# Probability-times-value matmuls in turn between two PSUM banks, in an attention and feed-forward kernel

## The chip, the cores and the metric

The kernel runs on one core of one Trainium2 chip. The metric is the device time of one execution in microseconds (us). Several executions of each kernel were timed; all that have a known state were in the fast state, with a granted TensorE clock of 0.997 to 1.000. Single looks on one core have the state "unknown", and nothing below rests on their total time alone.

## The reference

The reference is one transformer block with modulated layer norms, sliding-window attention over a cache, and a gated feed-forward part. All inputs are bfloat16. Cut to what matters:

```
h = layernorm(x) * (1 + ca) + sa                 # x: 2048 x 1024
q = h @ wq                                        # 32 heads of 128
k, v = last 512 rows of the caches                # 4 groups, 8 heads share one
p = softmax(q @ k.T / sqrt(128))                  # per head: 2048 x 512
x = x + ga * ((p @ v) @ wo)
x = x + gb * feed_forward(layernorm(x) * (1 + cb) + sb)
```

The change touches only `p @ v`. The kernel handles 512 query rows at a time, so there are 4 x 32 = 128 pieces of work, called heads below.

## The kernel before

Per head, the exponentials of the scores lie in SBUF as `ex_s`, 4 key tiles of 128 keys x 512 queries. The values lie in `v_aug`: for each group of heads four slices (one per key tile), each a row of 128 values and a column of ones. The column of ones makes the 129th output column the sum of the exponentials. A row is 130 elements long, of which a matmul reads 129.

```python
VW = 130
v_aug = arena.at(OFF_VA, [GK, VW], BF16, [B_va])        # GK = 16 slices: 4 groups x 4
...
T.op(POOL, lambda: g.memset(v_aug[:, :, P:VW], 1.0), writes=[B_va])
...
def pv(i):
    ...
    for j in range(TPC):                                 # 4 blocks of 128 queries
        b = PVB + j // 2                                 # bank 5, 5, 6, 6
        for kt in range(KT):                             # 4 v slices, added up in PSUM
            mm(bank(b, P + 1, (j % 2) * 130), ex_s[es][:, kt, j * P:(j + 1) * P],
               v_aug[:, gk * KT + kt, 0:P + 1],
               kt == 0, kt == KT - 1, [B_ex[es], B_va, B_vg[gk]], PB[b])
    both = [PB[PVB], PB[PVB + 1]]
    # VectorE: reciprocal of the four sums, then one multiplication over both banks
    ...
```

The second argument of `mm` is the stationary operand (weights, loaded anew for each matmul: the trace before has 7778 weight loads and 7636 matmuls, a few matmul records being missing) and the third the moving operand, here a v slice. The two flags say "overwrite" (first of a block) and "last of a block". Both banks are waited for and drained together, before and after the change.

In the loop over heads, TensorE does for one head the query projection (8 matmuls of 512 columns), for another the scores (4 of 512 columns), and for a third these 16 matmuls of 129 columns.

The softmax here doesn't subtract the row's maximum and nothing guards it: scores larger than these inputs give would overflow.

Of the kernel before, what the change touches and what calls it, by code (L numbers as in the profile page):

```python
# [7 lines left out]
P = 128  # L8
# [122 lines left out]
def bass_adaLN_cond__sliding_block_cached__swiglu_ffn__prompt_kernel(  # L131
# [23 lines left out]
    KT = W // P  # L155
# [3 lines left out]
    TPC = CH // P  # L159
# [57 lines left out]
    def bank(b, n=512, off=0):  # L217
        return ps[:, b * 512 + off:b * 512 + off + n]
# [7 lines left out]
    def psap(off, dims):  # L226
        return bass.AP(tensor=ps_t, offset=off, ap=[[4096, P]] + dims)

    PB = [_Buf("bank%d" % b) for b in range(8)]
# [23 lines left out]
    PVB = 5  # L253
    XB = 7

    with nc.Block() as block:

        @block.gpsimd
        def _(g):
# [5 lines left out]
            def mm(out_ap, lhsT, rhs, start, stop, reads, bank_buf, skip=False):  # L265
                T.op(PE, lambda: TE.matmul(out_ap, lhsT, rhs, start=start, stop=stop, skip_group_check=skip),  # L266
                     reads=reads, writes=[bank_buf])
# [98 lines left out]
            v_aug = arena.at(OFF_VA, [GK, VW], BF16, [B_va])  # L366
            Q_k = [dq("q_k%d" % i) for i in range(Hkv)]
            Q_v = [dq("q_v%d" % i) for i in range(Hkv)]
            B_vg = [_Buf("vg%d" % i) for i in range(Hkv)]
# [217 lines left out]
            for idx in range(GK):  # L587
                b = SCB + 1 + idx // 8
# [18 lines left out]
            B_ex = [_Buf("ex%d" % i) for i in range(NEX)]  # L607
            ex_s = [arena.at(OFF_EX + i * 4 * KB, [KT, CH], BF16, [B_ex[i]]) for i in range(NEX)]
# [14 lines left out]
            def pv(i):  # L623
                ch, h = divmod(i, Hq)
                gk = h // rep
                es = i % NEX
                os_ = i % NOS
                for j in range(TPC):
                    b = PVB + j // 2
                    for kt in range(KT):  # L630
                        mm(bank(b, P + 1, (j % 2) * 130), ex_s[es][:, kt, j * P:(j + 1) * P], v_aug[:, gk * KT + kt, 0:P + 1],
                           kt == 0, kt == KT - 1, [B_ex[es], B_va, B_vg[gk]], PB[b])
                both = [PB[PVB], PB[PVB + 1]]
                r = i % 2
                T.op(DVE, lambda: V.reciprocal(rl[r][:, :].rearrange("p (a b) -> p a b", a=2), psap(PVB * 512 + P, [[512, 2], [130, 2]])),  # L635
                     writes=both + [B_rl[r]])
                rlb = bass.AP(tensor=rl[r][:, :].tensor, offset=0, ap=[[4, P], [2, 2], [1, 2], [0, P]])
                T.op(DVE, lambda: V.tensor_tensor(o_s[os_].rearrange("p (a b) d -> p a b d", a=2),  # L638
                                                  psap(PVB * 512, [[512, 2], [130, 2], [1, P]]), rlb, ALU.mult),
                     reads=[B_rl[r]], writes=both + [B_os[os_]])  # L640
                T.op(Q_tr[os_], lambda: SP.dma_start_transpose(oT_all[:, h, :].rearrange("p (j q) -> p j q", j=TPC),
                                                               o_s[os_].rearrange("p j d -> p (j d)")),
                     reads=[B_os[os_]], writes=[B_oT[h]])
# [55 lines left out]
            for i in range(1, NA + 2):  # L699
# [35 lines left out]
                if 0 <= i - 2 < NA:  # L735
                    pv(i - 2)
                    ch2, h2 = divmod(i - 2, Hq)
                    if h2 == Hq - 1 and ch2 < NCH - 1:
                        finish(rows)
                        oproj(ch2)  # L740
# [144 lines left out]
```

## Time and profile before

| | before |
|---|---|
| time, median | 1291.36 us (3 executions, 1290.51 to 1291.66; the profiled one took 1292.6) |
| TensorE busy | 1265.6 of 1290.8 us |
| 2048 matmuls of 129 columns, busy | 140.6 us |
| heads apart | 3.52 us |

The page of the profile before, its first line, the busy times, and the line of the chain that ended last (shares of the span by engine). In the views that follow, L266 is the helper that issues nearly all matmuls:

```profile
span 1290.8 us, 17912 instructions
...
PE 1265.6 (98%) x7636; PEld 651.7 (50%) x7778; DVE 447.7 (35%) x823; ACT 341.3 (26%) x384; POOL 37.3 (3%) x94
...
PE 97%; issue 1%; DVE 1%; ACT 0%; DMA 0%; SPq 0%; POOL 0%; ACTq 0%
```

The groups of instructions by shape, before. The columns after the bar are busy us in total and mean ns of one, then the idle time of the engine before them:

```profile
L266 PE MATMUL ps<-arena 128*128 128x512 bf16 x5084 | 1134.8, 380 | 10.9 <-DVE arena L467 2.2 <-ACT arena L620 0.6 <-DVE tmp L657 0.4
L266 PEld LDWEIGHTS ps<-arena 128*128 128x128 bf16 x7346 | 637.4, 98 | 624.9 <-issue 7.9 <-ACT arena L620 1.6 <-DVE tmp L657 0.9
...
L266 PE MATMUL ps<-arena 128*128 128x129 bf16 x2048 | 140.6, 220 | 1.1 <-DVE arena L638 1.1
```

The timeline before, VectorE alone, the reciprocals of three heads in a row (start us, duration us):

```profile
403.46 0.18 DVE L635 RECIPROCAL rl<-ps 128x4 f32<-128x4 f32 x1 [1.10 <-PE ps L266]
...
406.98 0.18 DVE L635 RECIPROCAL rl<-ps 128x4 f32<-128x4 f32 x1 [1.10 <-PE ps L266]
...
410.50 0.18 DVE L635 RECIPROCAL rl<-ps 128x4 f32<-128x4 f32 x1 [1.10 <-PE ps L266]
```

What to see: TensorE is the bound, and the 129-column matmuls waited for another engine once, for 1.1 us in all. So whatever they cost is inside their own stream. Their mean duration of 220 ns says nothing of their cost, because matmuls overlap (their starts, below, are only 55.8 to 60.8 ns apart); 140.6 us / 2048 = 69 ns is nearer, but still has the tail of each run of 16 in it. What a matmul costs in a stream is the distance from its start to the next start.

These distances are worked out from the matmul records of the trace, as a mean over the 128 heads (for the last position, without the heads after which the record of the next matmul is missing from the trace). Each number is the distance from the matmul named to the next one, in ns; b is the bank and v the slice:

```
before   b5v0 b5v1 b5v2 b5v3 | b5v0 b5v1 b5v2 b5v3 | b6v0 b6v1 b6v2 b6v3 | b6v0 b6v1 b6v2 b6v3 | sum
         56.6 60.8 59.3 59.3 | 55.8 59.7 59.2 59.6 | 55.8 59.6 59.2 59.2 | 55.8 59.2 59.2 59.1 | 937.4
```

The 512-column matmuls are 215.8 ns apart. The first of each four is followed sooner than the others, by about 3.4 ns.

### The profile page before, as it was taken

To read this page: it belongs to the slowest core of one execution; us is meant where nothing else is said; L and a number is where in the kernel's file an instruction comes from. 1 tells how busy PE (TensorE), PEld (TensorE's weight loads), DVE (VectorE), ACT (ScalarE), POOL (GpSimd) and SP (SyncE) were. 2 spreads that over 40 slices of the span, in tenths; PEclk is the share of its full clock that TensorE was granted. 3 is DMA by queue.
4 is the path that set the end of the run, shared out by engine and by line. 5 is a ranking of instruction groups with operands and counts; after the bars stand their busy time and mean duration, and the time that the engine had idled before them with its cause. 6 is when DMAs were issued, how large, how long until landed. Compare 5 with 4: busy or idle time off the path is not lost.

```text
span 1290.8 us, 17912 instructions
## 1 busy us (share of the span) xinstructions
PE 1265.6 (98%) x7636; PEld 651.7 (50%) x7778; DVE 447.7 (35%) x823; ACT 341.3 (26%) x384; POOL 37.3 (3%) x94
## 2 busy tenths in 40 slices
PE   6999999999999999999999999999999999999999
PEld 3565545556445564456544444444444444444444
DVE  3455423654136542265422332233222331221222
ACT  2555402555015551055620111001100111001100
POOL 1001200000000000000000000000000000000000
PEclk9999999999999999999999999999999999999999
DMA  8989800844105541046340683045420564044300
GB/s 261 304 222 285 235 1 21 184 111 107 37 5 127 133 118 46 1 116 122 70 152 15 205 302 131 17 130 162 151 71 19 157 208 131 17 135 142 131 9 25
DMA packets 212592, 155.33 MB, mean 120 GB/s; under 512 B 104736, under 2 KB 199840, under 8 KB 211488
## 3 DMA queue, kind: packets, MB, share of 16 engines
q1 hardware_dynamic: 212512, 154.17, 42.4%
q8 instruction: 61, 1.00, 0.3%
q14 instruction: 19, 0.16, 0.0%
HBM read 125.83 MB, written 4.19 MB: 101 GB/s over the span
## 4 chain that ended last, share of the span: by engine, by line
PE 97%; issue 1%; DVE 1%; ACT 0%; DMA 0%; SPq 0%; POOL 0%; ACTq 0%
PE ps L266 97%; DMA x_res<-in_A_x_dram 0%; ACT arena L620 0%; PE ps L270 0%; DVE tmp L657 0%; DVE arena L467 0%; DVE st L388 0%; ACT L620 0%; ACT arena L489 0%; SPq L309 0%; DVE nsc L399 0%; DVE arena L638 0%; DVE x_res L659 0%; ACT arena L593 0%; DVE rl L635 0%
## 5 line engine op out<-in xcount | busy, mean ns | idle before, releaser
L266 PE MATMUL ps<-arena 128*128 128x512 bf16 (+1 forms) x7204 | 1251.5, 333 | 12.0 <-DVE arena L467 2.2
L266 PEld LDWEIGHTS ps<-arena 128*128 128x128 bf16 x7346 | 637.4, 98 | 624.9 <-issue 7.9
L620 ACT ACTIVATE arena<-ps 128x1024 bf16<-128x1024 f32 x256 | 261.7, 1023 | 358.9 <-PE ps L266 347.2
L815 ACT ACTIVATE arena<-ps 128x512 bf16<-128x512 f32 x112 | 66.9, 597 | 514.5 <-PE ps L266 511.6
L816 DVE TENSOR_TENSOR arena<-ps,arena 128x512 bf16<-128x512 f32 x112 | 77.5, 692 | 276.2 <-PE ps L266 276.2
L657 DVE TENSOR_TENSOR tmp<-ps,rowb 128x512 f32<-128x512 f32 (+1 forms) x65 | 44.4, 683 | 320.5 <-PE ps L266 320.5
L571 DVE CAST arena<-ps 128x512 bf16<-128x512 f32 x124 | 85.8, 692 | 65.5 <-PE ps L266 65.5
L638 DVE TENSOR_TENSOR arena<-ps,rl 128x512 bf16<-128x512 f32 x128 | 88.5, 691 | 4.4
L635 DVE RECIPROCAL rl<-ps 128x4 f32<-128x4 f32 x128 | 23.4, 183 | 149.7 <-PE ps L266 149.7
L388 DVE BATCH_NORM_STATS2 st<-x_res 128x6 f32<-128x512 bf16 x62 | 42.4, 684 | 4.3 <-DMA x_res<-in_A_x_dram 4.2
L393 POOL TENSOR_SCALAR rstd<-mv 128x1 f32<-128x1 f32 x31 | 7.0, 227 | 955.2 <-DVE mv L392 943.7
L659 DVE TENSOR_TENSOR arena<-tmp,x_res 128x512 bf16<-128x512 f32 (+1 forms) x33 | 22.3, 676 | 1.1
L659 DVE TENSOR_TENSOR x_res<-tmp,x_res 128x512 bf16<-128x512 f32 x32 | 22.1, 692 | 1.1
L404 DVE TENSOR_SCALAR arena<-arena,gain,mod_bf 128x512 bf16<-128x512 bf16 x56 | 20.4, 406 | 0.0
L395 POOL TENSOR_TENSOR rstd<-rstd,mhalf 128x1 f32<-128x1 f32 x31 | 17.7, 572 | 2.6
L399 DVE TENSOR_SCALAR nsc<-x_res,mv,rstd 128x1024 bf16<-128x1024 bf16 x30 | 16.1, 536 | 2.1 <-POOL rstd L395 2.1
L270 PE MATMUL ps<-arena,nsc 128*128 128x128 bf16 x16 | 2.1, 311 | 10.4 <-DVE nsc L399 10.2
L266 PEld LDWEIGHTS ps<-sc_bf,arena 128*128 128x128 bf16 x384 | 11.3, 97 | 0.5
L266 PE MATMUL ps<-sc_bf,arena 128*128 128x1 bf16 x384 | 11.5, 164 | 0.0
L540 POOL TENSOR_SCALAR arena<-arena,c 128x128 bf16<-128x128 bf16 x16 | 9.7, 621 | 36.0 <-PE ps L266 35.9
L392 DVE BATCH_NORM_AGGREGATE mv<-st 128x2 f32<-128x12 f32 x31 | 6.5, 209 | 1.1
L270 PEld LDWEIGHTS ps<-arena,nsc 128*128 128x128 bf16 x16 | 1.5, 142 | 10.4 <-DVE nsc L399 10.4
(37 smaller groups left out, 30.9 us busy)
## 6 DMA issues: line engine op xcount, KB each, us to landing
arena<-in_A_wq_dram SPq DMA_DIRECT2D x31, 1024.0 KB, 5.9
arena<-in_B_w_gate_dram SPq DMA_DIRECT2D x28, 1024.0 KB, 5.3
arena<-in_B_w_up_dram SPq DMA_DIRECT2D x28, 1024.0 KB, 7.4
arena<-in_w_mod_dram SPq DMA_DIRECT2D x8, 1024.0 KB, 7.2
arena<-in_A_wo_dram SPq DMA_DIRECT2D x8, 1024.0 KB, 8.2
arena<-in_B_w_down_dram SPq DMA_DIRECT2D x7, 1024.0 KB, 6.3
arena<-in_w_mod_dram SPq DMA_DIRECT2D x8, 512.0 KB, 7.8
out_dram<-arena SPq DMA_DIRECT2D x15, 256.0 KB, 2.0
```

Of the source, the lines that this page charges most:

```text
L266: T.op(PE, lambda: TE.matmul(out_ap, lhsT, rhs, start=start, stop=stop, skip_group_check=skip), reads=reads, writes=[bank_buf])
L388: T.op(DVE, lambda: V.bn_stats(st_[sl][:, hf * 6:hf * 6 + 6], x_res[:, t, hf * 512:hf * 512 + 512]), reads=[B_x[t]], writes=[B_st[sl]])
L395: T.op(POOL, lambda: g.tensor_tensor(rstd[sl][:, :], rstd[sl][:, :], mhalf[:, 0:1], ALU.pow), reads=[B_rs[sl], B_mh], writes=[B_rs[sl]])
L404: T.op(DVE, lambda: V.tensor_scalar(dst[:, dt, :], dst[:, dt, :], gain[gi][:, dt:dt + 1], mod_bf[:, ccol + dt:ccol + dt + 1], op0=ALU.mult ...
L571: T.op(DVE, lambda: V.tensor_copy(qT_s[qs], bank(QB)), writes=[PB[QB], B_qT[qs]])
L620: T.op(ACT, lambda: A.activation(ex_s[es][:, 2 * kp:2 * kp + 2, :], banks2(SCB + 2 * kp), AF.Exp, scale=att_scale), writes=[PB[SCB + 2 * k ...
L635: T.op(DVE, lambda: V.reciprocal(rl[r][:, :].rearrange("p (a b) -> p a b", a=2), psap(PVB * 512 + P, [[512, 2], [130, 2]])), writes=both + ...
L638: T.op(DVE, lambda: V.tensor_tensor(o_s[os_].rearrange("p (a b) d -> p a b d", a=2), psap(PVB * 512, [[512, 2], [130, 2], [1, P]]), rlb, A ...
L657: T.op(DVE, lambda: V.tensor_tensor(tmp[s][:, 0:n], bank(b, n), rowb[ri][:, c0:c0 + n], ALU.mult), reads=[B_row[ri]], writes=[PB[b], B_tmp ...
L659: T.op(DVE, lambda: V.tensor_tensor(dst[:, c0:c0 + n], tmp[s][:, 0:n], x_res[:, t, c0:c0 + n], ALU.add), reads=[B_tmp[s], B_x[t]], writes= ...
L815: T.op(ACT, lambda: A.activation(sg_s[ss], bank(gb), AF.Silu), writes=[PB[gb], B_sg[ss]])
L816: T.op(DVE, lambda: V.tensor_tensor(guT[:, ft, :], bank(ub), sg_s[ss], ALU.mult), reads=[B_sg[ss]], writes=[PB[ub], B_gu[ft]])
```

## The change

Its intent is to keep a matmul from adding onto the block that the matmul just before it wrote. Now two blocks, in bank 5 and in bank 6, are added to in turn.

```diff
-                for j in range(TPC):
-                    b = PVB + j // 2
+
+                for jj in range(2):
                     for kt in range(KT):
-                        mm(bank(b, P + 1, (j % 2) * 130), ex_s[es][:, kt, j * P:(j + 1) * P], v_aug[:, gk * KT + kt, 0:P + 1],
-                           kt == 0, kt == KT - 1, [B_ex[es], B_va, B_vg[gk]], PB[b])
+                        for jb in range(2):
+                            j = 2 * jb + jj
+                            b = PVB + jb
+                            mm(bank(b, P + 1, jj * 130), ex_s[es][:, kt, j * P:(j + 1) * P], v_aug[:, gk * KT + kt, 0:P + 1],
+                               kt == 0, kt == KT - 1, [B_ex[es], B_va, B_vg[gk]], PB[b])
```

There is a side effect: each v slice is now streamed twice in a row, once for each bank. The order of the slices was 0, 1, 2, 3, 0, 1, 2, 3 and is now 0, 0, 1, 1, 2, 2, 3, 3.

## The prediction

> **What bounds the kernel.** TensorE. The profile's chain of waits that ended last is 97% TensorE matmuls; the engine table has TensorE busy for 1265.6 of 1290.8 us at a granted clock of 1.00 from slice 2 on. The waits list shows almost nothing that TensorE waits for after the first 30 us (a few us in all), while VectorE and ScalarE wait for TensorE. So only time taken out of, or put into, the matmul stream itself can count.
>
> **What the change touches.** Per head (128 heads) the 16 probability-times-value matmuls (129 columns each, four accumulating onto each of four blocks). The instructions, operands, weight loads, sums and waits stay the same; only the order does. Before: four matmuls in a row add onto one block. After: the matmuls alternate between bank 5 and bank 6, so one other matmul stands between two additions to the same block. Both banks were already held until the end of the head and drained together, so no VectorE or ScalarE step is released sooner in kind.
>
> **Cost, from the trace.** I took start-to-start distances of consecutive matmul records. 512-column matmuls: 215.8 ns, 256-column: 109.2 ns. [...] For 129 columns the distance after the first matmul of each block (it overwrites) is 55.8 ns, but after each of the three that add it is about 59.2 ns (60.8 once, in the first block). So there are 12 x about 3.4 ns = about 41 ns per head above the 55.8 ns floor. Heads are 3.523 us apart (reciprocals in the timeline): 12 x 215.8 ns for the projection and scores, plus about 937 ns for these 16.
>
> Theory A: an addition onto a block written by the matmul just before has to wait a little for that write (about 59 ns from one start to the next[...]). Alternating banks makes the distance some 112 ns, and the excess vanishes: 128 x 41 ns = 5.2 us, all on the critical path, because TensorE is.
> Theory B: the excess comes from something else that goes with the second to fourth matmul of a block, such as the start of their v slices in SBUF (rows of 130 elements, so only every fourth slice starts on a 16-byte multiple). Then the order doesn't matter and nothing changes.
> I give A 0.6, B 0.35, and 0.05 to a small loss by switching banks. A loss is unlikely: the score matmuls switch banks at every instruction at 215.8 ns, without a visible cost.
>
> **Prediction.** With A about 1286.2 us, with B about 1291.3 us. I record 1287.0 us, 1284.8 to 1292.0. Faster by over 2%: 0.005; within 2%: 0.985; slower by over 2%: 0.01.
>
> **What would show it.** Right: the 129-column distances fall to about 56 ns at all positions, the heads come about 3.483 us apart, the group of 128x129 matmuls loses about 5 us of busy time (140.6 to about 135.5), and the 512-column group (1134.8 us), the idle times and the clock stay. Under B the distances stay at 59.2 ns after the slices 1 to 3 (now in pairs), and at 55.8 ns after slice 0.
>
> **What would make it wrong.** A cost of alternating that shows only for short matmuls, such as more than 59 ns per bank switch;[...] or a weight-load limit just below 59 ns that caps the gain.

128 x 41 ns = 5.2 us and the recorded 1287.0 us rest on distances in the trace before.

## The result, and the profile after

| | before | after |
|---|---|---|
| time, median of 4 | 1291.09 us | 1289.65 us |
| range | 1290.51 to 1291.66 | 1289.23 to 1290.84 |

The ratio is 0.999 (95% interval 0.9973 to 1.0008). It is worked out from the fast runs, and is not quite the ratio of the medians quoted. In a second set of rounds on another occasion (e11 below) it was 0.9982 (0.9969 to 0.9996). So the change gives 1.2 us in the first set (difference of the means) and 2.1 us in the second. The first interval includes no change at all; the second just excludes it.

The page after, the lines that answer to those shown of before:

```profile
span 1289.0 us, 17912 instructions
...
PE 1263.4 (98%) x7636; PEld 648.3 (50%) x7778; DVE 447.5 (35%) x823; ACT 341.3 (26%) x384; POOL 37.3 (3%) x94
...
PE 97%; DMA 1%; issue 1%; DVE 1%; SPq 0%; ACT 0%; POOL 0%; DVEq 0%
```

The groups by shape, after:

```profile
L266 PE MATMUL ps<-arena 128*128 128x512 bf16 x5084 | 1134.7, 380 | 11.7 <-DVE arena L467 2.2 <-DMA arena<-in_B_w_up_dram 0.8 <-ACT arena L620 0.7
L266 PEld LDWEIGHTS ps<-arena 128*128 128x128 bf16 x7346 | 634.0, 98 | 626.8 <-issue 7.1 <-ACT arena L620 1.6 <-DMA arena<-in_B_w_up_dram 1.6
...
L266 PE MATMUL ps<-arena 128*128 128x129 bf16 x2048 | 138.5, 220 | 1.1 <-DVE arena L641 1.1
```

The timeline after, two reciprocals in a row:

```profile
404.94 0.18 DVE L638 RECIPROCAL rl<-ps 128x4 f32<-128x4 f32 x1 [1.09 <-PE ps L266]
...
408.45 0.18 DVE L638 RECIPROCAL rl<-ps 128x4 f32<-128x4 f32 x1 [1.09 <-PE ps L266]
```

What to see: the 129-column group lost 140.6 - 138.5 = 2.1 us, and TensorE's busy time as a whole fell by 2.2 us. The 512-column group is the same. The heads are 3.51 us apart instead of 3.52. In the profiled run of after, TensorE's matmuls also had one wait for the load of `w_up`, 0.8 us. In before only a weight load waited for it, 0.2 us, and in e11, the same kernel again, nothing did; so it is not put down to the change. With it DMA rises from 0% to 1% in the chain that ended last.

The distances in the trace after, in the same form as above:

```
after    b5v0 b6v0 b5v1 b6v1 b5v2 b6v2 b5v3 b6v3 | b5v0 b6v0 b5v1 b6v1 b5v2 b6v2 b5v3 b6v3 | sum
         56.6 56.1 61.3 55.9 59.4 55.3 60.0 56.0 | 55.8 55.7 61.2 56.0 59.6 55.3 59.9 55.9 | 920.2
```

Here lies the surprise. If the delay came from adding onto a block just written (theory A), bank 5 and bank 6 would behave alike, and neither would show a delay. But the first matmul on slice 1, 2 or 3 still has it and the second on the same slice has not. If it came from where a slice starts (theory B), both would have it. Neither theory of the prediction gives this pattern.

### The profile page after: what moved, and what is told of

Read it like the earlier page. It is cut to its first block, busy times and chain, and to the rows that moved or that the text cites. A ratio compares the mean times of both kernels' runs of the same rounds, so it can differ in the third digit from the quotient of the medians.

```text
span 1289.0 us, 17912 instructions
## 1 busy us (share of the span) xinstructions
PE 1263.4 (98%) x7636; PEld 648.3 (50%) x7778; DVE 447.5 (35%) x823; ACT 341.3 (26%) x384; POOL 37.3 (3%) x94
## 4 chain that ended last, share of the span: by engine, by line
PE 97%; DMA 1%; issue 1%; DVE 1%; SPq 0%; ACT 0%; POOL 0%; DVEq 0%
PE ps L266 96%; DMA arena<-in_B_w_up_dram 1%; DMA x_res<-in_A_x_dram 0%; PE ps L270 0%; ACT arena L620 0%; DVE tmp L660 0%; DVE nsc L399 0%; DVE arena L467 0%; DVE st L388 0%; SPq L418 0%; ACT arena L489 0%; SPq L309 0%; DVE arena L641 0%; DVE x_res L662 0%; DVE rl L638 0%
## 5 line engine op out<-in xcount | busy, mean ns | idle before, releaser
(37 smaller groups left out, 30.8 us busy)
```

## The experiments

**A third theory.** A row of v is 260 bytes long and a matmul reads the first 258 of them. Counted from the start of a group's four slices, in lines of 16 bytes: slice 0 ends in line 16 (bytes 256 to 271), and slice 1 starts at byte 260, in the same line 16. Likewise slice 2 starts in the line where slice 1 ends, and slice 3 where slice 2 ends. Slice 3 to slice 0 and a slice to itself don't share a line. (How many lines one matmul touches can't be the cause: 258 bytes touch 17 of them from each of the four starts.) Theory C: a matmul is delayed where its moving operand starts in the 16-byte line in which that of the matmul before it ended. The line and its 16 bytes were the assumption at this point; what the runs show of them is worked out below the table of all runs.

Before has 3 such shared lines in each of 4 blocks, 12 per head. After has 6, because each slice runs twice and only the first of the pair follows another slice. Theory C was formed after the first four runs below; the expectations of those four speak of A and B alone.

Every kernel below gives the reference's result within the tolerance, but that test is blunt here: e2, which is wrong, passed it too.

### e1: the slices of a block in the order 1, 2, 3, 0

```diff
-                    for kt in range(KT):
+                    for kt in (1, 2, 3, 0):
...
-                           kt == 0, kt == KT - 1, ...
+                           kt == 1, kt == 0, ...
```

> The order of before, but each block of four runs its v slices in the order 1, 2, 3, 0 instead of 0, 1, 2, 3 (same result). It separates 'first matmul of a block' from 'slice 0'. Theory A (an addition waits for the write just before it): 55.8 ns after the first matmul of a block, now slice 1, and 59.2 ns after slices 2, 3 and 0. Theory B (where the v slice starts): 59.2 ns after slices 1, 2 and 3, and 55.8 ns after slice 0, which is now the last of its block. Heads stay 3.52 us apart under both.

Measured: in the second to fourth block 59.3 to 59.6 ns after slice 1, though it is the first of its block and overwrites, 59.1 to 59.3 after 2 and 3, and 55.8 to 55.9 after slice 0, though it adds. The pattern goes with the slice and not with the place in the block. Only in the first block, where slice 1 follows a 512-column matmul, is it 56.6 after slice 1. Theory A falls. Theory C counts 11 shared lines here (the first slice 1 of a head follows no slice 0), and the sum is 933.7 ns against 937.4, somewhat less as it should be.

### e2: all value matmuls overwrite (a wrong result)

```diff
-                           kt == 0, kt == KT - 1, [B_ex[es], B_va, B_vg[gk]], PB[b])
+                           True, True, [B_ex[es], B_va, B_vg[gk]], PB[b])
```

> The order of before, but every value matmul overwrites its block instead of adding (a wrong result on purpose). Theory A: no addition, no excess: all distances 55.8 ns, heads 3.483 us apart. Theory B: nothing changes: 59.2 ns after slices 1 to 3, heads 3.523 us apart.

Measured: 937.5 ns per 16 matmuls, against 937.4 before, with the same pattern at every position. Adding in PSUM costs nothing here. Theory A falls a second time.

### e3: rows of v of 132 elements

```diff
-            VW = 130
+            VW = 132
```

> The order of before, with v rows of 132 elements instead of 130 (264 bytes), so that slices 0 and 2 of a group start on a multiple of 16 bytes and slices 1 and 3 eight bytes past one. Theory A: no change, 59.2 ns after slices 1, 2 and 3. Theory B: 55.8 ns after slices 0 and 2, about 59.2 ns after slices 1 and 3; heads 3.497 us apart (two thirds of 41 ns less one third: 27 ns of excess left).

Measured: 55.8 to 55.9 ns after slices 0 and 2 (56.6 for the first of a head), 59.2 to 60.8 after slices 1 and 3, sum 924.4, heads 3.513 us apart (median). The pattern is that of theory B. The figure for the heads in the expectation was a slip: with 14 ns less, they should have come 3.509 us apart, not 3.497. Theory C gives the same pattern, because with rows of 264 bytes slices 1 and 3 share a line with the slice before and slice 2 doesn't. This run alone can't tell B and C apart.

### e4: rows of v of 136 elements

The edit is the same with 136. Now every slice starts on a multiple of 16 bytes.

> The order of before, with v rows of 136 elements (272 bytes), so that every slice starts on a multiple of 16 bytes. Theory A: no change, 1291.1 us. Theory B: 55.8 ns at all positions, heads 3.483 us apart, 5.2 us less: about 1286 us, faster than the change (1289.65 us).

Measured: 56.6 to 56.7 ns at every position, sum 906.6, ratio to before 0.9969 (0.9955 to 0.9983), median 1288.37 us. The whole pattern is gone without a change of order or bank. The distance is 56.7 and not the 55.8 ns expected, so the gain per head is 31 ns and not 41.

The group of the 129-column matmuls in e4, of the groups by shape:

```profile
L266 PE MATMUL ps<-arena 128*128 128x129 bf16 x2048 | 137.0, 220 | 1.1 <-DVE arena L638 1.1
```

### e5: the changed kernel with rows of 136

The changed kernel, with `VW = 136`.

> The order of after (two banks in turn) with v rows of 136 elements. Theory B (a start off a 16-byte multiple costs 3.4 ns) and theory C (a matmul is delayed where it starts in the same 16-byte line in which the matmul just before it ended; with rows of 130, slice 1 starts in the line where slice 0 ends, and so on) both leave the order nothing to do: 56.7 ns at all positions as in e4, 1288.4 us. If alternating has a gain of its own, it is lower than e4.

Measured: 56.6 to 56.7 ns everywhere, sum 906.7, ratio to before 0.9977 (0.9965 to 0.9990). In the trace it is e4 to 0.1 ns. With no shared line, alternating the banks gives nothing.

### e6: rows of 130, the slices in the order 0, 2, 1, 3

```diff
-                    for kt in range(KT):
+                    for kt in (0, 2, 1, 3):
...
-                           kt == 0, kt == KT - 1, ...
+                           kt == 0, kt == 3, ...
```

> The kernel before (rows of 130, no alternating), with the slices of a block in the order 0, 2, 1, 3, so that no matmul starts in the line where the one before it ended, while the starts stay off the 16-byte multiples. Theory B: 59.2 ns after slices 2, 1 and 3, nothing gained, 1291.1 to 1292.4 us like before. Theory C: no excess anywhere, about 55.8 ns at all positions, heads about 3.483 us apart, about 5 us less than before.

Measured: sum 907.5 ns, heads 3.497 us apart (median), ratio 0.9974 (0.9960 to 0.9988). The starts off 16-byte multiples are still there, and the cost is gone, so theory B falls. The positions weren't as expected, however: in each block 59.1 after slice 2 and 55.8 to 55.9 after the others (56.6 for the first of a head). The four make 55.8 + 59.1 + 55.8 + 55.9 = 226.6 ns, the same as four times 56.65 in e4. So a single distance is not the cost of one matmul; the sum over a block is. The group of the 129-column matmuls in e6 is at the level of e4 (137.0 us):

```profile
L266 PE MATMUL ps<-arena 128*128 128x129 bf16 x2048 | 136.9, 219 | 1.1 <-DVE arena L638 1.1
```

The 55.8 ns that the prediction took for a floor is only the fast part of such a pattern.

### e7: rows of 130, the slices in the order 3, 2, 1, 0

> As e6, with the order 3, 2, 1, 0: again no start in the line where the matmul before ended. Theory B: 59.2 ns after slices 3, 2 and 1, 55.8 ns after 0. Theory C: no excess, about 55.8 ns everywhere.

Measured: sum 909.4 ns; 60.0 after slice 3 and 55.8 to 56.1 after the others, from the second block on. The sum has no excess as large as before's, as C has it, but the even distances expected are there in the first block alone (56.6 to 56.7), and 2.8 ns per head more than in e4 stay unexplained.

### e8: rows of v of 134 elements

> The order of before with v rows of 134 elements (268 bytes). Slices 1, 2 and 3 all start off a 16-byte multiple (12, 8 and 4 bytes past one), but only slice 1 starts in the line where the matmul before it ended. Theory B: 59.2 ns after slices 1, 2 and 3. Theory C: an excess (about 59.2 ns) after slice 1 only; heads about 3.496 us apart.

Measured: 60.8 ns after slice 1, 55.8 to 56.2 after the others (56.6 for the first of a head), sum 915.1, heads 3.504 us apart. This is the sharpest test of what must coincide. Slice 1 starts with 10 bytes between it and the end of slice 0 (byte 268 after byte 257), in the same line; slice 2 has the same 10 bytes before it (536 after 525), but starts in the next line. Only the first has the delay. Single distances can mislead (e6), but the sum says the same: it is 8.5 ns above e4's, 2.1 per block, which is the excess of one delayed matmul and not of three. So it is the shared line, not the nearness and not the start as such. The group in e8, between that of e4 and that of before:

```profile
L266 PE MATMUL ps<-arena 128*128 128x129 bf16 x2048 | 137.9, 219 | 1.1 <-DVE arena L638 1.1
```

### e9: the banks in turn, the slices as before

```diff
-                for j in range(TPC):
-                    b = PVB + j // 2
-                    for kt in range(KT):
-                        mm(bank(b, P + 1, (j % 2) * 130), ...
-                           kt == 0, kt == KT - 1, ...
+                for jj in range(2):
+                    for jb, kt in ((0, 0), (1, 1), (0, 2), (1, 3), (1, 0), (0, 1), (1, 2), (0, 3)):
+                        j = 2 * jb + jj
+                        b = PVB + jb
+                        mm(bank(b, P + 1, jj * 130), ...
+                           kt == jb, kt == 3 - jb, ...
```

> Rows of 130. The banks alternate as in after (two places per eight matmuls excepted, where two in a row go to one bank, on different slices), but the v slices follow each other 0, 1, 2, 3, 0, 1, 2, 3 as in before: 12 starts per head in the line where the matmul before ended, like before. Theory A (what helps is another bank): the distances and heads of after, or better (about 918 ns per 16 matmuls, heads 3.508 us apart). Theory C: those of before (about 936 ns, 3.524 us).

Measured: sum 937.4 ns, that of before to 0.1 ns, and heads 3.525 us apart (median), as in before. The banks were alternated and nothing was gained.

### e10: the slices in pairs as after, in one bank

```diff
-                for j in range(TPC):
-                    b = PVB + j // 2
+                for jb in range(2):
                     for kt in range(KT):
-                        mm(bank(b, P + 1, (j % 2) * 130), ...
-                           kt == 0, kt == KT - 1, ...
+                        for jj in range(2):
+                            j = 2 * jb + jj
+                            b = PVB + jb
+                            mm(bank(b, P + 1, jj * 130), ...
+                               kt == 0 and jj == 0, kt == KT - 1, ..., skip=True)
```

Two blocks of one bank are now open at once. The author let only the first matmul of the bank carry the "overwrite" flag (`skip=True` turns off the program's own check of these flags). Whether that is needed, and whether the sums come out right with it, is not shown: no run sets the flag otherwise here, and the blunt test above, which e10 passed, can't vouch for either. e10 is read for its times alone.

> Rows of 130. The slices come in pairs as in after (0, 0, 1, 1, 2, 2, 3, 3), but into two blocks of one bank; the bank changes only once per head. 6 shared lines per head, like after. Theory A: no gain over before from banks (about 936 ns per 16 matmuls), unless other columns of one bank are enough. Theory C: the distances of after, about 918 to 920 ns, heads 3.508 us apart, with the excess after the first matmul of the pairs of slices 1, 2 and 3.

Measured: sum 920.3 ns, after's to 0.1 ns, and heads 3.509 us apart (median), as in after. All the gain of the change was had without alternating banks.

The group of the 129-column matmuls, of the groups by shape, in e9:

```profile
L266 PE MATMUL ps<-arena 128*128 128x129 bf16 x2048 | 140.6, 220 | 1.1 <-DVE arena L639 1.1
```

and in e10:

```profile
L266 PE MATMUL ps<-arena 128*128 128x129 bf16 x2048 | 138.5, 220 | 1.1 <-DVE arena L640 1.1
```

What to see: 140.6 us is the busy time of before and 138.5 us that of after. The pair e9 and e10 takes the change apart into its two halves, and the whole effect goes with the order of the slices.

### e11 and e12: the change and the longer rows, in one set of rounds

> The changed kernel again, on the same chip as e12, for a direct comparison. About 2.2 us less than before: ratio about 0.998.

> e4 again (order of before, rows of 136), beside e11. Theory C: 12 shared lines removed against 6, about 3.5 us less than before and about 1.5 us less than e11: ratio about 0.997.

Measured against the same nine runs of before (median 1291.69 us): the change 1290.17 us median, ratio 0.9982 (0.9969 to 0.9996); rows of 136 in the old order 1288.69 us, ratio 0.9971 (0.9958 to 0.9983). The differences of the means are 2.1 and 3.7 us. The trace says 128 x 17.2 ns = 2.2 us and 128 x 30.8 ns = 3.9 us. The traces tell the two kernels clearly apart (920.4 against 906.6 ns per head); the intervals of the two ratios overlap. The five times of each, taken in the same rounds on one chip, don't: 1288.99 to 1290.38 us for the change, 1287.15 to 1288.74 us for the rows of 136.

### All runs by shared lines

Worked out from the traces: the sum of the 16 distances, mean over heads, and what it exceeds e4's 906.6 by:

| kernel | rows of | banks in turn | shared lines per head | sum, ns | excess, ns | per shared line |
|---|---|---|---|---|---|---|
| before | 130 | no | 12 | 937.4 | 30.8 | 2.6 |
| e9 | 130 | nearly always | 12 | 937.4 | 30.8 | 2.6 |
| e2, all overwrite | 130 | no | 12 | 937.5 | 30.9 | 2.6 |
| e1, order 1 2 3 0 | 130 | no | 11 | 933.7 | 27.1 | 2.5 |
| e3 | 132 | no | 8 | 924.4 | 17.8 | 2.2 |
| after (e11: 920.4) | 130 | yes | 6 | 920.2 | 13.6 | 2.3 |
| e10 | 130 | no | 6 | 920.3 | 13.7 | 2.3 |
| e8 | 134 | no | 4 | 915.1 | 8.5 | 2.1 |
| e7, order 3 2 1 0 | 130 | no | 0 | 909.4 | 2.8 | - |
| e6, order 0 2 1 3 | 130 | no | 0 | 907.5 | 0.9 | - |
| e5 | 136 | yes | 0 | 906.7 | 0.1 | - |
| e4 (e12: 906.6) | 136 | no | 0 | 906.6 | 0 | - |

The excess follows the count of shared lines at 2.1 to 2.6 ns each, over three ways of changing the count (row length, order of slices, pairing) and whatever the banks do. The runs also fix the size of the line. If the count is redone with another power of two, it no longer fits. Lines of 8 bytes can't be shared in all three places where before has the delay; lines of 32 bytes or more would still be shared in e4, which has none.

## Why the prediction was right or wrong

**Right, and what of it was luck.** The time lay in the range and within 2%. That is luck as far as the mechanism goes: the range, 1284.8 to 1292.0 us, held both theories and even no change at all (1291.09 us), and neither theory was right. What was right by its reasoning: TensorE's stream was what counted (its busy time fell by 2.2 us); the 512-column group (1134.8 and 1134.7 us) and the clock (0.999 in both traces) stayed; the excess over the floor was the right thing to look at; no cost of switching banks showed (937.4 ns in e9 as in before).

**Wrong: the likelier cause, theory A** ("an addition onto a block written by the matmul just before has to wait a little for that write"). The overwriting kernel e2 has the same excess (937.5 ns against 937.4), and e9 alternates the banks and gains nothing (937.4). The first matmul of a block looked fast because it is the one on slice 0, and slice 0 is the one that shares no line with the slice before it (in e1, where it comes last in its block, it still has 55.8 to 55.9 ns). Two things went together in the trace before (first of the block, slice 0), and the prediction gave the wrong one 0.6.

**Half wrong: theory B** ("the start of their v slices in SBUF"). The place in SBUF is the cause, but not in the form given. Starts off a 16-byte multiple cost next to nothing by themselves (e6: 907.5 ns per head against 906.6 in e4; slices 2 and 3 of e8: 55.8 to 56.2 ns). What costs is to start in the line where the matmul before ended (2.1 to 2.6 ns each time in the table). And so its conclusion, "Then the order doesn't matter and nothing changes", failed: the order decides how often lines are shared. The change halved that count, 12 to 6, as a side effect.

**Mis-sized: the gain**, "128 x 41 ns = 5.2 us". With all excess gone the 16 matmuls take 906.6 ns and not 16 x 55.8 = 893, because 55.8 ns is only one step of an uneven pattern; so at most 30.8 ns per head were to be had, 3.9 us. Of this the change took 17.2 ns, 2.2 us in the trace. The recorded 1287.0 us lay between the figures of two theories, each of which was wrong; the measured 1289.65 us lies between what the two gave (1286.2 and 1291.3), for a reason that neither had.

**What stays open.** The runs show when the delay comes, not how the hardware makes it. Why a shared line costs 2.6 ns where there are twelve and 2.1 where there are four, why slice 2 in e6 and slice 3 in e7 carry a long step, and the 2.8 ns left in e7, are not explained. Lines are counted from the start of the v buffer, whose own address no run shows. The delays themselves say where it lies: the counts of the table come out only if it starts on a multiple of 16 bytes, or 2 bytes after one.

## What to carry to other kernels

When short matmuls stream neighbouring slices of one SBUF buffer and TensorE is the bound, try rows that are a multiple of 16 bytes long (here 136 elements instead of 130, at no cost in instructions), or an order in which no slice starts in the line where the last one ended. In the traces this gave 3.9 us (e4) and 3.8 us (e6) per execution, 0.3% of the time, against 2.2 us for the change under study. It is shown here for 129 columns of bfloat16 alone. Before giving a regular pattern in the trace to one cause, list all that repeats with the same period, and look for a run that moves one of them alone. An experiment that does only the named half of a change (e9) and one that does only its side effect (e10) settle what a dozen timings of the whole can't.
